# Loading the last batch's q, k and v in three whole transfers, turning one batch on TensorE, and doubling a row buffer in a planned attention-and-mixer kernel

## The chip, the cores and the metric

The kernel runs on one core of a Trainium2 chip. The metric is the device time of one execution in microseconds (us); lower is better. Three runs of the kernel before took 182.30, 182.91 and 182.94 us, median 182.91.

A core has TensorE (PE, matrix products into PSUM, eight banks of 128 x 512 floats), VectorE (DVE), ScalarE (ACT), GpSimd (POOL) and SyncE (SP). Here POOL also issues nearly all loads, since they cast float32 to bf16 on the way, and SP issues the stores, the first loads and all small transfers inside the chip's SBUF memory. Each engine runs its own instructions strictly in order; between engines there are only semaphores.

## What is computed

Four batches of a gated linear attention (8 heads of 48, 768 positions) feed a mixer with a token part and a channel part:

```python
f = sigmoid(f_logit)
for t in range(768):                       # per batch and head
    state = f[t][:, None] * state + outer(k[t], v[t])
    y[t] = q[t] @ state
x = y as (batch, 768, 384)
h = relu(x.T @ w_tok1) @ w_tok2            # over positions
u = x + h.T
out = u + relu(u @ w_ch1) @ w_ch2          # over the 384 channels
```

## The kernel before, in words

**Attention.** A batch is cut into six chunks of 128 positions. `gates` takes `f_logit` through Exp and Ln on ACT and splits the result into two bf16 parts; the subtraction that makes the lower part, `Llo` (L484), runs on DVE for batches 0 and 1, on DVE or POOL for batch 2, on POOL for batch 3. `sums_and_turns` forms running sums over the chunk with a triangular matrix on PE (L553, L554), their exponentials `G` and `Gi` on ACT (L564, L566), scales q and k in one DVE product (L586), and turns the result to `qkT`: on PE with a DVE copy (L603, L616), for batch 3 with a DMA transpose from SP (L593). The last row of the sums is needed down the partitions. ACT writes it to a row of `ends` (L573), and four transfers of SP per chunk (L580) carry it to `glast`, which the state update reads (L649, L652, L654 on DVE). Two copies then put the state into `state_bd` as bf16 (L458 on ACT or L462 on POOL). `attention` handles two chunks at a time: scores (L503), a chunk's own contribution to the state (L519), then per chunk the masking `AmT` (L640) and the output y, from the earlier state (L671) and from within the chunk (L678). It goes to `x_bf` and `x_nat`.

**Mixer.** `mixer` does, per batch: the token part (L708 with `w_tok1`, relu to `h1T` on ACT or DVE; L724 with `w_tok2`), `u` into `x_nat` (L740 on DVE) and as bf16 into `u_bf` (ACT or POOL), the turn of `u` to `uT` in two halves of three tiles, the channel part's first product (L783, 24 groups of three matmuls, relu to `zT` on ACT L467 or DVE L469) and its second (L802, six tiles of twelve matmuls, the last addition on DVE at L808, the store on SP at L812). For a batch listed in `U_TURNED` each half of `uT` is one DMA transpose from SP (L754); otherwise it is nine PE transposes (L765) with three copies out of PSUM (L460).

**Loads.** `load` issues one chunk of one tensor from POOL (L400), 1024 rows of 48 numbers. `load_pair` issues two chunks of f, then k, q, v of each. The buffers of q, k, v are three deep over batches, those of f two, so batch 3 goes into batch 0's q, k, v and batch 1's f. POOL takes its loads in the order in which they are added, and a subtraction or a copy that stands between two loads on POOL holds the later ones.

**The order.** Nothing is issued in source order. Every operation is put into a list (`Plan.add`) with its engines, a rank, what it needs and makes, and an assumed cost; `Plan.order` runs through a model of the engines and hands out operations by earliest start plus lag, then rank, and chooses the engine where an operation may run on several. The table `SHIFTS` overrides rank and lag of several hundred operations by their number in the list. So the position of almost every instruction on every engine follows from the table, and matmuls on a constant tile (L849) fill PE's idle time in the first 25 us.

Below, "batch 2 chunk 5" and the like name these pieces. "Filler" is what PE can do while something else is late, above all the second channel product of the batch before. Line numbers are those of the kernel before; the changed kernel's lines past the table stand six or seven higher.

Of the kernel before, what the change touches and what calls it, by code (L numbers as in the profile page):

```python
# [10 lines left out]
FP32 = mybir.dt.float32  # L11
# [8 lines left out]
U_TURNED = (2,)  # L20
TURNED = 3
SHIFTS = (
# [63 lines left out]
)  # L86
KEPT = 3
SPLIT = 5
# [211 lines left out]
def kernel(  # L300
# [12 lines left out]
    nc = tc.nc  # L313
# [91 lines left out]
    def load_w(name, dst, src, size):  # L405
        add(POOL, 5.0,
            lambda: nc.gpsimd.dma_start(out=dst, in_=src.rearrange("(kt p) n -> p kt n", p=128)),
            make=[name], kind=("load", 900, 1024, size, 8000))
# [424 lines left out]
    for b in range(B):  # L833
# [8 lines left out]
        if b == 1:  # L842
            for c in range(0, NCH, 2):
                load_pair(3, c)
# [38 lines left out]
```

## Time and profile before

| | |
|---|---|
| median of three runs | 182.91 us |
| the profiled execution's own time | 182.56 us |
| its span in the profile | 180.9 us, so 1.66 us lie around it |
| PE busy | 165.9 us (92%) |
| DVE, ACT, POOL busy | 126.3, 122.5, 100.8 us |
| TensorE clock granted | 0.998 |
| POOL's loads by chunk (L400) | 90, about 0.93 us each of POOL's time |
| small transfers to `glast` (L580) | 60, median 4.0 us from issue to landing |
| DMA transposes | 2 of `uT`, 6 of `qkT` |

A busy PE means that at least one matmul is in flight; a matmul of 384 columns is recorded with 0.32 us but the next starts 0.163 us later (28 in 4.71 us). The timeline merges neighbouring instructions of a line. A note in brackets at the end of a line gives the engine's idle time before it and what ended it.

### The profile page before, as it was taken

Reading aid. Unit: us, or ns where it says so; the run is one execution under the profiler, and the core shown is the slowest. Engines: PE = TensorE matmul, PEld = TensorE weight load, DVE = VectorE, ACT = ScalarE, POOL = GpSimd, SP = SyncE. Lnnn points to the kernel's source line nnn. Section 1 sums busy time; section 2 is a strip of 40 time slices with the busy share of each in tenths; the row PEclk is TensorE's granted clock in tenths of the full one; section 3 lists DMA queues with packets and bytes.
Section 4 is the critical chain, followed back from the end, with each engine's and each line's share of the span. In section 5 each row is a group of like instructions: output and inputs, shape, how many; then the busy total and the mean of one; then the engine's idle time right before and its main releaser. Section 6 shows DMA issues by size and latency. Waiting matters only on the chain.

```text
span 180.9 us, 4340 instructions
## 1 busy us (share of the span) xinstructions
PE 165.9 (92%) x1630; PEld 104.3 (58%) x1634; DVE 126.3 (70%) x274; ACT 122.5 (68%) x277; POOL 100.8 (56%) x136
## 2 busy tenths in 40 slices
PE   6978998899989999899999969859999999999992
PEld 2445655566656666566666545536667666656662
DVE  6669995876878998899997978345789455601222
ACT  4578984889869699989989569737827325494100
POOL 7999478795599949879999907420211111000000
PEclk9999999999999999999999999999999999999999
DMA  7999999999999999999999915994395010300132
GB/s 102 137 171 156 147 173 176 202 135 230 131 170 146 210 210 121 153 113 53 159 158 110 182 46 68 106 164 102 64 180 177 4 43 0 124 12 0 43 132 89
DMA packets 106645, 22.15 MB, mean 122 GB/s; under 512 B 99360, under 2 KB 105760, under 8 KB 106624
## 3 DMA queue, kind: packets, MB, share of 16 engines
q0 software_dynamic: 79440, 13.77, 96.7%
q1 hardware_dynamic: 27184, 8.10, 23.0%
q8 instruction: 13, 0.21, 0.5%
q14 instruction: 8, 0.07, 0.1%
HBM read 25.17 MB, written 4.72 MB: 165 GB/s over the span
## 4 chain that ended last, share of the span: by engine, by line
PE 53%; DMA 15%; DVE 11%; ACT 11%; issue 4%; SPq 2%; POOL 1%; ACTq 0%; DVEq 0%; POOLq 0%
PE ps L783 22%; PE ps L802 15%; DMA glast<-ends 8%; DMA uT<-u_bf 4%; DVE AmT L640 3%; PE ps L724 3%; DMA f_sb<-in_f_logit_dram 3%; SPq L580 2%; DVE state L654 2%; ACT state_bd L458 2%; PE ps L708 2%; DVE x_nat L740 2%; PE ps L603 2%; PE ps L765 2%; PE ps L503 2%
## 5 line engine op out<-in xcount | busy, mean ns | idle before, releaser
L783 PE MATMUL ps<-uT,w_ch 128*128 128x384 bf16 x288 | 51.4, 326 | 2.7 <-DMA uT<-u_bf 2.7
L802 PE MATMUL ps<-w_ch,zT 128*128 128x384 bf16 (+2 forms) x300 | 51.8, 320 | 0.0
L467 ACT ACTIVATE zT<-ps 128x384 bf16<-128x384 f32 x72 | 33.9, 491 | 18.4 <-PE ps L783 16.3
L783 PEld LDWEIGHTS <-w_ch 128*128 128x128 bf16 x288 | 27.4, 98 | 20.3 <-issue 2.9
L802 PEld LDWEIGHTS <-zT 128*128 128x128 bf16 x300 | 27.8, 98 | 16.6
L640 DVE TENSOR_TENSOR AmT<-ps,tri_bf 128x512 bf16<-128x512 f32 x46 | 30.2, 684 | 3.8 <-PE ps L503 3.6
L400 POOL DMA_DIRECT2D v_sb<-in_v_dram x24 | 22.2, 927 | 4.5 <-DMA w_ch<-in_moe_w_ch_dram 4.5
L808 DVE TENSOR_TENSOR x_nat<-x_nat,ps 128x384 f32<-128x384 f32 (+2 forms) x25 | 13.3, 535 | 14.3 <-PE ps L802 14.1
L400 POOL DMA_DIRECT2D qk_sb<-in_k_dram x24 | 22.5, 938 | 1.3 <-POOLq L867 0.8
L400 POOL DMA_DIRECT2D qk_sb<-in_q_dram x24 | 22.3, 927 | 0.0
L469 DVE TENSOR_SCALAR zT<-ps 128x384 bf16<-128x384 f32 x24 | 12.9, 554 | 9.8 <-PE ps L783 9.6
L586 DVE TENSOR_TENSOR qk<-qk_sb,GG 128x768 bf16<-128x768 bf16 (+1 forms) x30 | 14.2, 481 | 4.1 <-ACT GG L566 2.2
L400 POOL DMA_DIRECT2D f_sb<-in_f_logit_dram x18 | 16.6, 952 | 0.4 <-DMA f_sb<-in_f_logit_dram 0.2
L478 ACT ACTIVATE f_sb<-f_sb 128x384 f32<-128x384 f32 x24 | 12.5, 520 | 4.6 <-DMA f_sb<-in_f_logit_dram 4.4
L462 POOL CAST state_bd<-state 48x192 bf16<-48x192 f32 x13 | 4.5, 344 | 18.9 <-DVE state L654 9.8
L849 PE MATMUL ps<-steady 128*128 128x512 bf16 x36 | 11.6, 435 | 1.9 <-DVE steady L432 1.5
L458 ACT ACTIVATE state_bd<-state 48x192 bf16<-48x192 f32 x27 | 9.8, 361 | 5.0 <-DVE state L654 4.3
L566 ACT ACTIVATE GG<-ps 128x384 bf16<-128x384 f32 x24 | 11.5, 489 | 1.3 <-PE ps L554 0.9
L564 ACT ACTIVATE GG<-ps 128x384 bf16<-128x384 f32 x24 | 11.6, 487 | 0.9 <-PE ps L554 0.7
L603 PE MATMUL ps<-ident,qk 128*128 128x128 bf16 x144 | 11.7, 220 | 0.6 <-DVE qk L586 0.2
L603 PEld LDWEIGHTS <-qk 128*128 128x128 bf16 x144 | 8.9, 98 | 5.4 <-DVE qk L586 4.0
L740 DVE TENSOR_TENSOR x_nat<-x_nat,ps 128x384 f32<-128x384 f32 x21 | 10.7, 550 | 1.2 <-PE ps L724 1.0
(75 smaller groups left out, 242.9 us busy)
## 6 DMA issues: line engine op xcount, KB each, us to landing
out_dram<-x_nat SPq DMA_DIRECT2D x23, 192.0 KB, 2.0
f_sb<-in_f_logit_dram POOLq DMA_DIRECT2D x18, 192.0 KB, 5.6
qk_sb<-in_k_dram POOLq DMA_DIRECT2D x24, 96.0 KB, 5.2
qk_sb<-in_q_dram POOLq DMA_DIRECT2D x24, 96.0 KB, 5.4
v_sb<-in_v_dram POOLq DMA_DIRECT2D x24, 96.0 KB, 5.5
f_sb<-in_f_logit_dram SPq DMA_DIRECT2D x6, 192.0 KB, 4.7
w_ch<-in_moe_w_ch_dram POOLq DMA_DIRECT2D x2, 576.0 KB, 9.8
w_ch<-in_moe_w_ch_dram POOLq DMA_DIRECT2D x1, 1152.0 KB, 10.2
```

The source lines that it names most:

```text
L400: lambda eng=eng, into=into, of=of: eng.dma_start(out=into, in_=of),
L458: nc.scalar.activation(out_, in_, AF.Copy, bias=0.0, scale=1.0)
L467: nc.scalar.activation(out_, in_, AF.Relu, bias=0.0, scale=1.0)
L469: nc.vector.tensor_scalar(out_, in_, 0.0, None, ALU.max)
L478: add(ACT, r, lambda: nc.scalar.activation(fb, fb, AF.Exp, bias=0.0, scale=-1.0), make=[key], kind=el)
L586: add(DVE, r, lambda n=n: nc.vector.tensor_tensor(qk[i4][:, n, :, 0:D], qk_sb[nb][:, n, :, c, :], GG[i][:, n], ALU.mult), need=[(x, nb, c) ...
L603: nc.tensor.transpose(to[:, o + hp, :], blk(src)[:, hp, :], ident)
L640: add(DVE, r, lambda half=half, made=made: nc.vector.tensor_tensor(half, made(), tb4, ALU.mult), need=["tri_bf"], make=[("AmT", i, p)], ba ...
L740: nc.vector.tensor_tensor(to, un, banks[pm.at][:, 0:DM], ALU.add)
L783: nc.tensor.matmul(banks[pm.at][:, 0:384], lhsT=w[:, kt, c0:c0 + 128], rhs=uT[:, th, :, kt, :], start=(kt == 0), stop=(kt == 2))
L802: nc.tensor.matmul(banks[pm.at][:, 0:n1 - n0], lhsT=zT[:, kt, tt * 128:(tt + 1) * 128], rhs=w_ch2[:, kt, n0:n1], start=(kt == 0), stop=(kt ...
L808: add(DVE, rank("ch2", tt), lambda un=un, pm=pm, n=n1 - n0: nc.vector.tensor_tensor(un, un, banks[pm.at][:, 0:n], ALU.add), make=[("x_nat" ...
```

## The change

Four edits, and a new table:

- `U_TURNED` is empty, so batch 2's `u` is turned by PE.
- Batch 3 is loaded as six chunks of f, then k, q and v whole: three transfers of 6144 rows in place of eighteen of 1024.
- `ends` has four buffers in place of two, so the row of chunk c no longer waits for the transfers of chunk c-2.
- `SHIFTS` is new throughout. (Its numbers also refer to a list that has become three entries shorter.)

```diff
-U_TURNED = (2,)
+U_TURNED = ()
 TURNED = 3
 SHIFTS = (
-    (38,-50,4900), (51,50,3800), (54,300,6100), (87,60,2600), (90,90,400), (91,90,1000), (93,120,800),
...
+    (19,30,1600), (24,60,700), (39,-50,5800), (42,-50,4500), (48,-50,3700), (52,50,4200), (56,300,2900),
...
-    ends = [st([128, H, 64], FP32, f"ends{i}") for i in range(2)]
+    ends = [st([128, H, 64], FP32, f"ends{i}") for i in range(4)]
...
+    def load_whole(b):
+        for n in "kqv":
+            dst, src = names[n]
+            i = b % len(dst)
+            add(POOL, 30.0, lambda into=dst[i], of=src[b].rearrange("h (c t) d -> t h c d", t=C):
+                nc.gpsimd.dma_start(out=into, in_=of), make=[(n, i, c) for c in range(NCH)],
+                kind=("load", 2250, 128 * H * NCH, 4450, 8000))
...
-                ends[i][96:128, :, 0:D], sview()[96:128], AF.Exp, bias=0.0, scale=-1.0),
-                make=[("ends", i)], bank=p_s, kind=el)
+                ends[g4][96:128, :, 0:D], sview()[96:128], AF.Exp, bias=0.0, scale=-1.0),
+                make=[("ends", g4)], bank=p_s, kind=el)
...
-                row = ends[i][127:128].rearrange("o (hp par) d -> o hp (par d)", par=2)
+                row = ends[g4][127:128].rearrange("o (hp par) d -> o hp (par d)", par=2)
...
         if b == 1:
-            for c in range(0, NCH, 2):
-                load_pair(3, c)
+            for c in range(NCH):
+                load("f", 3, c)
+            load_whole(3)
         mixer(b, ranks(b))
```

`g4` is `(b * NCH + c) % 4`, the number that `glast` already uses. In the built programs PE has 18 transposes more and 3 fill matmuls fewer, DVE 8 copies, 7 relus and 2 memsets more and 2 subtractions fewer, ACT 10 instructions fewer, POOL 15 transfers fewer and 2 subtractions and 1 copy more, SP 2 transposes fewer.

More of the change, by code (lines that the diff above doesn't have):

```diff
@@ L439 @@
         once(DVE, lambda i=i: nc.vector.memset(state_bd[i], 0.0), [("sbd", i)], 220)
+    for i in range(4):
         once(DVE, lambda i=i: nc.vector.memset(ends[i][96:128, :, D:64], 1.0), [("ends", i)], 200)
-    for i in range(4):
         for n, tl in (("qh", qh[i]), ("kh", kh[i])):
@@ L573, in sums_and_turns @@
             add(ACT, r, lambda: nc.scalar.activation(
-                ends[i][96:128, :, 0:D], sview()[96:128], AF.Exp, bias=0.0, scale=-1.0),
-                make=[("ends", i)], bank=p_s, kind=el)
+                ends[g4][96:128, :, 0:D], sview()[96:128], AF.Exp, bias=0.0, scale=-1.0),
+                make=[("ends", g4)], bank=p_s, kind=el)
             def across():
-                row = ends[i][127:128].rearrange("o (hp par) d -> o hp (par d)", par=2)
+                row = ends[g4][127:128].rearrange("o (hp par) d -> o hp (par d)", par=2)
                 for hp in range(HP):
                     nc.sync.dma_start(out=glast[g4][:, hp:hp + 1], in_=row[:, hp])
-            add(SP, r, across, need=[("ends", i)], make=[("glast", g4)],
+            add(SP, r, across, need=[("ends", g4)], make=[("glast", g4)],
                 kind=("fix", 1900, (7000, 7000, 4500)[b - 1], 520))
```

122 rows, old and new, of the table SHIFTS are left out of this document.

## The prediction

> **What bounds the kernel.** I read the page's slices first, then PE's timeline for its gaps, the waits, and each gap's cause in the other engines' rows.
>
> ```profile
> PE   6978998899989999899999969859999999999992
> ```
>
> PE is full in nearly every slice of 4.5 us past the start. What stays short is the start (chained through loads, ACT and DVE), slices 23 to 26 (104 to 122 us), and the end. So past 30 us a change pays only by what it takes out of PE's gaps, less what it adds to PE's work. The long gaps in PE's timeline:
>
> ```profile
> 53.32 0.33 PE L671 MATMUL ps<-state_bd,qkT 128*128 128x96 bf16 x4 [0.82 <-ACT state_bd L458]
> 73.92 2.33 PE L724 MATMUL ps<-h1T,w_tok 128*128 128x384 bf16 x12 [0.46 <-ACT h1T L467]
> 105.44 0.33 PE L671 MATMUL ps<-state_bd,qkT 128*128 128x96 bf16 x4 [1.55 <-ACT state_bd L458]
> 112.33 4.71 PE L802 MATMUL ps<-w_ch,zT 128*128 128x384 bf16 x28
> 119.70 4.55 PE L783 MATMUL ps<-uT,w_ch 128*128 128x384 bf16 x27 [2.65 <-DMA uT<-u_bf]
> ```
>
> Others past 30 us are below 0.3 each but one of 0.49; from 119.70 to the last matmul none is listed. The two big ones, 4.20 us together, have their causes here:
>
> ```profile
> 101.01 3.38 POOL L484 TENSOR_TENSOR Llo<-f_sb 128x384 bf16<-128x384 f32 x4
> 102.18 2.44 DVE L654 TENSOR_TENSOR state<-tsum,glast 128x192 f32<-128x192 f32 x1
> 104.65 0.74 ACT L458 ACTIVATE state_bd<-state 48x192 bf16<-48x192 f32 x2 [2.50 <-DVE state L654]
> 112.13 1.90 SPq L754 DMA_TRANSPOSE uT<-u_bf  x1
> ```
>
> A state update that takes 0.36 elsewhere lasts 2.44 while POOL runs four subtractions, so ACT's copies and PE's y of batch 2 chunk 5 are late. Then the DMA transpose, issued at 112.13, lands 7.53 later (the chain has that piece); PE works off 28 matmuls of batch 1 and idles.
>
> **The change, part by part**, against the profiled execution's 182.56. Positions in the changed kernel are from its built order, times by stepping through the pitches of these rows.
>
> *PE turns u of batch 2.* The 2.65 goes: the nine transposes of a half come right after the bf16 copies of u, then 0.35 per copy out of PSUM, and the filler left (12 matmuls before the turns, 8 behind, 20 x 0.163 = 3.3) covers additions, copies and turns. It adds 18 transposes; the chain has nine at batch 3 in 0.50, so +1.0 of PE time, in a stretch that is full. The six DVE copies (six took 1.67 in batch 1) lie beside those 8 and the first L783 groups; uncovered they cost the 1.67. On SP 3.9 of issuing go, for whose followers (transposes of `qkT`) PE does not wait now. Net -1.65; bounds -1.65 and +0.1.
> The Trainium skill ("TensorE: Matmul & The Clock Gate", Part 4: PE-mode transpose) gives about 275 ns for a turn in a kernel; by it 18 would be 4.95 and the sum 185.2. The trace has 0.055 each, pipelined, and decides.
>
> *The late state update.* POOL again has four subtractions of batch 3 in a row (chunks 1, 2, 0, 5), but behind the issue of whole q and, by ACT's order, with gaps; the last state update comes by my steps after them. I take -1.4; bounds -1.55 (gone) and +0.5 (again, and a second run of two in batch 2, whose last subtractions move from DVE to POOL).
>
> *Whole loads: POOL's time.*
>
> ```profile
> 23.16 1.54 POOL L407 DMA_DIRECT2D w_ch<-in_moe_w_ch_dram  x2
> 36.00 1.01 POOL L407 DMA_DIRECT2D w_ch<-in_moe_w_ch_dram  x1
> 84.40 1.80 POOL L400 DMA_DIRECT2D f_sb<-in_f_logit_dram  x2
> ```
>
> The first have 384 rows and take 0.77, a chunk has 1024 and takes 0.90, the last weight 1536 and takes 1.01: 0.208 ns a row. So 6144 rows are an estimated 1.97 (bound from above: six chunks' pitches of 0.87, 5.2). POOL saves 18 x 0.90 - 3 x 1.97 = 10.3, off the path. But half of the state copy for batch 2's last y, on ACT before, is on POOL now, behind the fourth subtraction and whole v: subtraction done at about 103.7, issue 2.0, copy 0.34, y at 106.1, where PE arrives at 105.7. +0.4; bounds 0 and +3.6 (issue 5.2). Behind that copy in POOL's line waits a tile of u_bf, not needed until 112.
>
> *Whole loads: landing.* Before, eight chunk loads start every 6.97 us (84.40, 91.37, 98.35) and land a steady 4.4 after issue, so a chunk drains in 0.87 or less. Two more subtractions and a copy stand in POOL's line ahead of batch 2's last q and v, waiting for ACT's Ln of chunk 5, so f of batch 3 starts near 88.5, not 84.40. Whole q is 18 chunks on: 88.5 + 17 x 0.87 + 4.4 = 107.7. The first product with q (L586) stands on DVE in front of the six additions of u; `G` for it is ready near 108.8. A margin of 1.1. I put +0.3; bounds 0 and +2.5 (at 1.05 a chunk q lands at 110.8, the additions come 2.0 later and PE's filler covers little). v lands by 114, y needs it near 120.
>
> *Four rows of `ends`.*
>
> ```profile
> ACT ends L573 <- DMA glast<-ends: 3.7, 4, 1.2
> ```
>
> ACT's four waits go, but it had no PE gap right behind them: the gap at 53.32 waits for `glast` itself, and the others fall where PE is full. 0; bound -0.5. Two more memsets (0.165 each) stand at 29 us, where DVE waits for PE; 0, or +0.17 if one meets `h1T`.
>
> *The new order.* Three spots. (1) Batch 1's second relu of `h1T` now stands on ACT behind G, Gi and the row of batch 2 chunk 1 (0.37 + 0.53 + 0.50, then 0.45) with 0.94 of PE work beside it: a gap of about 1.2 for 0.46, and two of 0.2 nearby that I no longer find: +0.5, bounds 0 and +0.9. (2) y of batch 1 chunk 1 waits for the same `glast`, but PE arrives with two L783 groups fewer done: +0.3, less 0.2 for a PE turn of batch 0 put off: +0.1, bounds -0.2 and +1.0. (3) The end:
>
> ```profile
> 177.11 0.69 DVE L808 TENSOR_TENSOR x_nat<-x_nat,ps 128x288 f32<-128x288 f32 x2 [0.50 <-PE ps L802]
> ```
>
> Before, the last tile is cut 288 + 96: the final addition takes 0.255, its store of 48 KB 1.6. The changed order does that tile first and ends with a whole one: addition 0.55, store of 192 KB 2.0 at the median. +0.3 + 0.2, hence +0.5, bounds +0.3 and +1.5 (slowest store 2.8). The 3 fill matmuls (0.65) went from PE time that waits anyway.
>
> Sum: -1.65 - 1.4 + 0.4 + 0.3 + 0.5 + 0.1 + 0.5 = -1.25: 181.3. The profiled execution lies 0.35 under the median of its kernel, which the forecast ignores; the comparison is with 182.91.
>
> **Rivals.**
> *A, slower: the whole loads hold up batch 2's u.* If f starts late or the three transfers drain at the 1.0 to 1.3 us a chunk that packet records of batch 3 often show, q lands at 110 to 115, and the DVE products, in order, stand before the six additions, `u_bf`, the turns and every L783 of batch 2. It decides once q lands after about 109.5; from there PE loses one for one. At 1.15 a chunk: 88.5 + 17 x 1.15 + 4.4 = 112.5, 3 later; 181.3 + 3 = 184.3, with POOL's issue at 3 instead of 2 near 185. For it: DMA is the busiest resource there. Against: landings did not lengthen in batch 3, and nothing but stores and small rows competes.
> *B, no change: the order gives it back.* The state updates are held off again and DVE, 13 instructions heavier, opens small PE gaps between 75 and 101, where before has only one of 0.28: 182.56 + 0.1 for the stall kept (-1.25 + 1.4) + 0.3 = 183.0. For it: that stretch has DVE and ACT above 90%, and any misjudged step shows. Against: the same work is only dealt out otherwise.
> The Trainium skill ("SBUF — State Buffer", Who interferes with whom) says that a DVE instruction with two SBUF inputs and a GpSimd one that reads SBUF shut each other out; the 2.44 row agrees, and by it two more subtractions on POOL speak for B.
> *C, more gain:* both gaps go, q is early, and spots (1) and (2) cost nothing: -1.65 - 1.55 + 0.4 + 0.5 = -2.3, and -0.5 for `ends`: 179.8.
> *The edits do not bite* is excluded: the built program has three whole transfers and no DMA transpose of u.
>
> **How the numbers follow.** Forecast 0.42, A 0.25, B 0.22, C 0.11. Predicted: 181.3. For 8 in 10 the range runs from C's far side to A's: 178.9 to 185.2; the forecast's own is 180.3 to 182.4. Of 182.91, 0.5% is 0.9 us, about what a measurement of this kernel can tell from no change: faster means below 182.0, slower above 183.8. Forecast gives 0.38 faster and 0.04 the same; C 0.11 faster; B 0.02, 0.17, 0.03; A slower: faster 0.51, same 0.21, slower 0.28.
>
> **What would show it.** PE's wait for `uT` absent and no idle over 0.5 before batch 2's first L783; whole issues near 2.0 on POOL; q landing before DVE's first batch-3 product (a DVE wait on that DMA means A); no L654 above 0.5 (else B); a wait of L724 on `h1T` near 1.2; PE's last matmul near 175.8 and 3.9 from it to the end of the span. Wrong if PE shows new gaps between 75 and 101 or after 120, where I count none.

## The result: slower, 184.89 us

| kernel | median | kernel before, same chip | ratio to before, 95% interval |
|---|---|---|---|
| changed | 184.89 us (5 runs, 183.81 to 185.98) | 182.55 us (5 runs) | 1.0147 [1.0102, 1.0192] |

The forecast was 181.3, faster. The time lies in its range, the sign is wrong. The ratio leaves disturbed executions out, here and in all that follows, and the medians do not, so the two need not agree to the last tenth.

The changed kernel's profiled execution took 184.89, of which its span is 183.1 (before: 182.56 and 180.9). From its page, the span, the engines' busy time and PE's slices:

```profile
span 183.1 us, 4353 instructions
...
PE 168.0 (92%) x1649; PEld 104.0 (57%) x1649; DVE 130.9 (71%) x289; ACT 117.8 (64%) x267; POOL 93.9 (51%) x124
...
PE   6897996899998999699999889999999999999991
```

PE is busy 2.1 us longer. The hollow at slices 23 to 26 is filled but for two eights, and a new 6 stands at slice 17 (73 to 78 us). PE's timeline in the changed kernel, with the idle time before a row and what ended it in brackets:

```profile
17.33 0.40 PE L609 MATMUL ps<-ident,qk 128*128 128x128 bf16 x4 [1.33 <-DVE qk L592]
...
35.64 4.55 PE L789 MATMUL ps<-uT,w_ch 128*128 128x384 bf16 x27
...
76.13 1.95 PE L730 MATMUL ps<-h1T,w_tok 128*128 128x384 bf16 x11 [1.53 <-ACT h1T L473]
...
100.83 0.33 PE L677 MATMUL ps<-state_bd,qkT 128*128 128x96 bf16 x4 [0.32 <-ACT state_bd L464]
...
102.88 0.62 PE L609 MATMUL ps<-ident,qk 128*128 128x128 bf16 x8 [0.41 <-DVE qk L592]
...
104.94 0.40 PE L509 MATMUL ps<-qkT 48*128 48x128 bf16 x8 [0.30 <-DVE qkT L622]
106.00 0.40 PE L509 MATMUL ps<-qkT 48*128 48x128 bf16 x8 [0.66 <-DVE qkT L622]
...
117.68 1.18 PE L771 MATMUL ps<-ident,u_bf 128*128 128x128 bf16 x18
...
120.00 1.14 PE L789 MATMUL ps<-uT,w_ch 128*128 128x384 bf16 x6
```

The wait of 2.65 for `uT` is gone: 18 transposes in 1.18 and, with filler between, the first hidden-layer product of batch 2 at 120.00 with no idle before it. The other big wait, 1.55 at 105.44, has become four small ones, 1.69 together. New are 1.33 near the start and 1.53 where 0.46 was (batch 1's second token product). What stands behind the four, in the rows of POOL, DVE and ACT:

```profile
90.74 5.31 POOL L398 DMA_DIRECT2D f_sb<-in_f_logit_dram  x6
...
98.20 2.29 POOL L408 DMA_DIRECT2D qk_sb<-in_q_dram  x1
100.43 1.69 POOL L490 TENSOR_TENSOR Llo<-f_sb 128x384 bf16<-128x384 f32 x2
104.87 1.79 POOL L490 TENSOR_TENSOR Llo<-f_sb 128x384 bf16<-128x384 f32 x2 [2.75 <-ACT f_sb L485]
...
98.65 0.90 DVE L660 TENSOR_TENSOR state<-tsum,glast 128x192 f32<-128x192 f32 x1
100.82 1.53 DVE L660 TENSOR_TENSOR state<-tsum,glast 128x192 f32<-128x192 f32 x1 [0.41 <-ACT state_bd L464]
102.28 0.54 DVE L592 TENSOR_TENSOR qk<-qk_sb,GG 128x768 bf16<-128x768 bf16 x1
...
109.77 0.35 DVE L660 TENSOR_TENSOR state<-tsum,glast 128x192 f32<-128x192 f32 x1
...
102.44 0.73 ACT L464 ACTIVATE state_bd<-state 48x192 bf16<-48x192 f32 x2 [1.29 <-DVE state L660]
```

It is the stall of before at another place: POOL starts two subtractions at 100.43, a state update (batch 2 chunk 3) comes at 100.82 and does not end until they have (102.12); all that is behind it on DVE, the q and k product first, is late. The last update of the batch, the one that was held before, comes at 109.77, clear of all four subtractions, and takes 0.35. Behind the 1.53 at 76.13 are these ACT rows, and behind the 1.33 at 17.33 this DVE row:

```profile
74.19 0.49 ACT L570 ACTIVATE GG<-ps 128x384 bf16<-128x384 f32 x1
74.57 0.48 ACT L572 ACTIVATE GG<-ps 128x384 bf16<-128x384 f32 x1
75.08 0.48 ACT L579 ACTIVATE ends<-ps 32x384 f32<-32x384 f32 x1
75.59 0.49 ACT L473 ACTIVATE h1T<-ps 128x384 bf16<-128x384 f32 x1
...
16.91 0.36 DVE L592 TENSOR_TENSOR qk<-qk_sb,GG 128x384 bf16<-128x384 bf16 x1 [1.25 <-DMA qk_sb<-in_k_dram]
```

The relu stands behind G, Gi and the row, as the prediction read from the order. The k product of batch 0's fourth chunk now stands on DVE ahead of work that is ready, and waits for its load.

Where the 2.2 us of the spans come from: 1.04 up to batch 0's first hidden-layer product (34.60, now 35.64); from there PE's listed waits fall from 6.18 to 4.59 (sums of the brackets) while 1.18 of transposes come, -0.4; from the end of the last matmul to the end of the span 3.39 has become 3.81, since a whole tile is stored last, +0.4. The remaining 1.2 or so is not in the listed waits. Between that first product and the last matmul PE is busy 136.41 of 142.91 us before and 138.54 of 143.65 after, so idle time outside the list grew by only 0.2 (0.32 to 0.52). The other 1.0 lies inside PE's busy time, where a late start need not show as idle (a matmul is recorded with 0.32 us, and the next can start after 0.163); no run traces it further.

### The profile page after: what moved, and what is told of

It reads as the page before. It is cut to its first block, busy times and chain, and to the rows that moved or that the text cites. A ratio compares the mean times of both kernels' runs of the same rounds, so it can differ in the third digit from the quotient of the medians.

```text
span 183.1 us, 4353 instructions
## 1 busy us (share of the span) xinstructions
PE 168.0 (92%) x1649; PEld 104.0 (57%) x1649; DVE 130.9 (71%) x289; ACT 117.8 (64%) x267; POOL 93.9 (51%) x124
## 4 chain that ended last, share of the span: by engine, by line
PE 50%; DMA 14%; ACT 8%; POOL 8%; DVE 8%; SPq 5%; issue 4%; DVEq 0%; POOLq 0%; ACTq 0%
PE ps L789 18%; PE ps L808 16%; DMA glast<-ends 9%; SPq L586 5%; POOL qk_sb L398 4%; DMA qk_sb<-in_k_dram 3%; PE ps L714 3%; PE ps L730 2%; ACT state_bd L464 2%; DMA qkT<-qk 2%; PE ps L509 2%; POOL v_sb L398 2%; PE ps L771 2%; DVE state L660 1%; PE ps L609 1%
## 5 line engine op out<-in xcount | busy, mean ns | idle before, releaser
L473 ACT ACTIVATE zT<-ps 128x384 bf16<-128x384 f32 x65 | 31.0, 490 | 17.8 <-PE ps L789 16.2
L475 DVE TENSOR_SCALAR zT<-ps 128x384 bf16<-128x384 f32 x31 | 16.0, 549 | 4.6 <-PE ps L789 4.6
L398 POOL DMA_DIRECT2D v_sb<-in_v_dram x18 | 16.5, 917 | 5.2 <-DMA w_ch<-in_moe_w_ch_dram 5.2
L398 POOL DMA_DIRECT2D qk_sb<-in_k_dram x18 | 16.6, 924 | 1.2 <-POOLq L874 0.8
L398 POOL DMA_DIRECT2D qk_sb<-in_q_dram x18 | 16.6, 921 | 0.0
L468 POOL CAST state_bd<-state 48x192 bf16<-48x192 f32 x15 | 5.1, 341 | 21.1 <-DVE state L660 13.0
L609 PE MATMUL ps<-ident,qk 128*128 128x128 bf16 x144 | 11.1, 220 | 2.6 <-DVE qk L592 2.5
L572 ACT ACTIVATE GG<-ps 128x384 bf16<-128x384 f32 x24 | 11.6, 490 | 1.0 <-PE ps L560 0.7
L464 ACT ACTIVATE state_bd<-state 48x192 bf16<-48x192 f32 x25 | 9.0, 360 | 5.1 <-DVE state L660 3.9
```

Of the source, the lines that this page charges most:

```text
L398: lambda eng=eng, into=into, of=of: eng.dma_start(out=into, in_=of),
L464: nc.scalar.activation(out_, in_, AF.Copy, bias=0.0, scale=1.0)
L473: nc.scalar.activation(out_, in_, AF.Relu, bias=0.0, scale=1.0)
L475: nc.vector.tensor_scalar(out_, in_, 0.0, None, ALU.max)
L609: nc.tensor.transpose(to[:, o + hp, :], blk(src)[:, hp, :], ident)
```

## The experiments

Theory "order": the three structural edits pay, and the new order that the table `SHIFTS` makes costs more than they bring. Rival "edits": the edits cost by themselves. To part them, the experiments have no table: the order of all operations, with engine and PSUM bank, is written out as a list, once as the kernel before has it and once as the changed kernel has it (with either list every engine's instructions and their order are those of the original), and one thing is edited by hand. The source is shorter there, so the lines differ: the state update is L572 to L575, POOL's subtraction L402 to L404, the state copy L376 to L381, the hidden-layer product L702 or L703, the turns of u L685. In the diffs names stand for the operations' numbers: 2.3 is batch 2, chunk 3.

### The old order with the edits put in, together and one by one

```diff
 # e1: all three; e2 the first, e3 the second, e4 the third alone
+DVE  memset ends[2], ends[3]                  behind the first memsets
-SP   DMA transpose uT, tiles 0-2 / tiles 3-5
+PE   9 transposes of u, tiles 0-2             among batch 1's second products (about 112 us)
+PE   9 transposes of u, tiles 3-5             among batch 2's first second products (about 127 us)
+DVE  3 copies to uT behind each nine
-POOL f3.0 f3.1 k q v, k q v, f3.2 f3.3 ...
+POOL f3.0 ... f3.5 at the places of the first six loads, then k3, q3, v3 whole
```

> The kernel before with its order kept instruction by instruction on every engine, and the three edits put into it by hand: batch 2's u turned by TensorE in two groups of nine transposes ahead of the hidden-layer products that read them, f of batch 3 by chunk and then k, q, v whole, four sets of ends rows. Theory 'order' (the loss of the changed kernel comes from the new order that its table of shifts makes, not from the edits): 180.3 to 182.2 us against about 182.5, ratio 0.988 to 0.998; the 2.65 us wait of TensorE for the u transfer is gone and nothing of its size takes its place. Theory 'edits' (the edits cost by themselves, through POOL's issues of 2.3 us, the added transposes and copies, or the two added memsets): 183.0 to 185.0 us, ratio 1.003 to 1.014.

> The order before, with four sets of ends rows and nothing else; two more memsets of about 0.17 us on VectorE, behind the first ones. Theory 'order': no change, ratio 0.998 to 1.002, and the first hidden-layer product of batch 0 starts at 34.6 us as before. Theory 'edits': the two memsets push the start, that product starts at 34.9 us or later, as in the changed kernel (35.6), and the time is 0.3 to 1.0 us longer.

> The order before, with batch 2's u turned by TensorE (18 transposes, six VectorE copies) and nothing else. Theory 'order': 2.65 us of waiting go, 1.2 us of transposes come, 180.8 to 181.8 us, ratio 0.991 to 0.997. Theory 'edits': the copies (six of about 0.35 us) hold up VectorE where it releases batch 3's first chunks, and the gain is given back: 182.2 to 183.5 us.

> The order before, with batch 3's f by chunk first and its k, q, v whole behind, and nothing else; the loads start at the places on POOL where the paired loads started. Theory 'order': between 0.5 us shorter and 0.5 us longer (POOL issues for 6.9 us in place of 16, the first f arrive 2 to 5 us earlier): ratio 0.997 to 1.003. Theory 'edits': the whole k and q arrive after the product that reads their first chunk, or the long issues hold up the state copies behind them: 183.3 to 184.5 us, ratio 1.004 to 1.011.

Measured, on one chip, beside 29 runs of the kernel before with a median of 182.10:

| run | median | ratio to before, 95% interval |
|---|---|---|
| e1, all three | 180.42 us (12 runs) | 0.9906 [0.9849, 0.9962] |
| e2, ends only | 182.77 us (6 runs) | 1.0126 [1.0053, 1.0200] |
| e3, turn only | 181.25 us (12 runs) | 1.0003 [0.9957, 1.0050] |
| e4, whole loads only | 181.11 us (12 runs) | 0.9991 [0.9948, 1.0035] |

The same edits that came with 1.0147 in the new order give 0.9906 in the old one. So the order costs 2.4% against the old one, some 4.4 us (the two intervals together leave an estimated 1.7 to 3.2%), and the edits bring 0.9%: "order" is borne out, "edits" falls. Alone, turn and whole loads are not told from no change by their ratios. For the whole loads that is what "order" expected; for the turn it is a miss, since 0.991 to 0.997 was expected. The four sets alone came out slower by their ratio (by the medians 0.4%), where both theories said nothing or little. Their six times fall into two groups of three, 181.58 to 181.86 and 183.68 to 183.97, and the profile is of one in the lower group, so it cannot show why (span 179.9 against 180.9, batch 0's first hidden-layer product at 33.62; the waits for `uT` are 1.93 and 0.96 where before had one of 2.65). A later pair of runs takes it up.

Why e4 gives little and e1 more can be read in part from the traces; for e3 it stays open. In e3's trace the wait for `uT` is gone and the wait of 1.56 at 105.54 stays; new is one of 1.34 for `state_bd` at 71.30, where before had 0.22. In e1 PE has no wait for `uT`, but the state update is held off again, through all four subtractions. Rows of POOL, DVE and PE in e1, and the POOL and DVE rows of e4 at the same place:

```profile
101.51 3.18 POOL L403 TENSOR_TENSOR Llo<-f_sb 128x384 bf16<-128x384 f32 x4
102.06 2.87 DVE L574 TENSOR_TENSOR state<-tsum,glast 128x192 f32<-128x192 f32 x1
105.74 0.33 PE L591 MATMUL ps<-state_bd,qkT 128*128 128x96 bf16 x4 [1.96 <-ACT state_bd L377]
...
101.19 3.32 POOL L402 TENSOR_TENSOR Llo<-f_sb 128x384 bf16<-128x384 f32 x4
102.26 0.79 DVE L573 TENSOR_TENSOR state<-tsum,glast 128x192 f32<-128x192 f32 x1
```

In e4 `u` still goes by transfer. From the view of the tile `uT` the time from issue to landing of the two transfers, and from PE's timeline the one wait left for them:

```profile
DMA to landing us min/median/max: 2.9/3.1/3.2
...
129.87 2.45 PE L702 MATMUL ps<-uT,w_ch 128*128 128x384 bf16 x14 [1.35 <-DMA uT<-u_bf]
```

Before, the two took 3.5 and 7.5 (the first one had five chunk loads, issued at 110.4 to 113.9, beside it). With whole loads both take about 3, and the wait ahead of batch 2's first product disappears with no turn by PE at all; but PE is then early for the second half and waits 1.35 there. The turn in e1 has neither. In e4's profiled execution the state update took only 0.79, since it got in behind the second of the four subtractions (0.83 each from 101.19; update from 102.26 to 103.05): the same order around it, another outcome, and why is not shown.

### The new order with one thing moved

```diff
 # a1
-ACT  G 2.1, Gi 2.1, ends 2.1, relu h1T 1.1
+ACT  G 2.1, Gi 2.1, ends 2.1
-DVE  relu h1T 1.0
+DVE  relu h1T 1.0, relu h1T 1.1
-PE   transposes 2.0, token product 1.1.5
+PE   token product 1.1.5, transposes 2.0
 # a2
-ACT  state copy 2.3, both halves
+ACT  state copy 2.3, one half
-POOL q3 whole, 4 subtractions of batch 3
+POOL q3 whole, state copy 2.3 (other half), 4 subtractions of batch 3
 # a3
-DVE  k product 0.3, qkT 0.2, tsum 0.1, state 0.1, x_nat 0.1, AmT 0.2, q product 0.3
+DVE  qkT 0.2, tsum 0.1, state 0.1, x_nat 0.1, AmT 0.2, k product 0.3, q product 0.3
```

In a3 the transposes of that k on PE and their copy on ACT go back with it.

> The changed kernel's order, one thing moved: batch 1's second h1T relu goes from ScalarE (behind two gate products and an ends row) to VectorE, right behind the first one, and the last of its six products on TensorE goes ahead of the eight transposes before it. Theory 'order': the wait of 1.53 us ahead of batch 1's second token product is gone or under 0.4 us, that product starts 1.0 to 1.5 us earlier against the first hidden-layer product of batch 0, and the whole is 0.7 to 1.3 us shorter than the changed kernel (183.6 to 184.2 where that takes 184.9). Theory 'edits': no more than 0.3 us of it is left at the end, since another wait behind takes it.

> The changed kernel's order, one thing moved: one half of the state copy behind batch 2's fourth chunk goes from ScalarE to POOL, ahead of the four subtractions of batch 3, so that POOL cannot start them before VectorE's state update is done. Theory 'order' with POOL's subtractions as what holds the update: that update takes 0.35 to 0.45 us in place of 1.53, and TensorE's waits at 100 to 106 us (0.32, 0.41, 0.30, 0.66) fall by 0.8 to 1.4 us together. Rival (the issue of the whole q, not the subtractions, holds the update): it stays above 0.9 us.

> The changed kernel's order, one thing moved: VectorE's k product of batch 0's fourth chunk (which waits 1.25 us for the k load) goes behind the third chunk's scores, with its transposes on TensorE and its copy on ScalarE. Theory 'order': the wait of 1.33 us on TensorE at 17.3 is gone, batch 0's first hidden-layer product starts at 34.4 to 35.0 us in place of 35.64. Rival (the start is set by when the loads land, whatever the order): 35.4 to 35.9 us, the wait goes to another instruction.

One execution each, so the traces count and not the totals (183.44, 182.32 and 184.09 us; the kernel before took 181.27 beside them). a2 first, in the rows of DVE and POOL:

```profile
100.23 0.36 DVE L574 TENSOR_TENSOR state<-tsum,glast 128x192 f32<-128x192 f32 x1 [0.96 <-ACT state_bd L377]
100.75 0.52 POOL L381 CAST state_bd<-state 48x192 bf16<-48x192 f32 x1 [0.84 <-DVE state L574]
101.35 3.18 POOL L403 TENSOR_TENSOR Llo<-f_sb 128x384 bf16<-128x384 f32 x4
```

The copy, which needs the update's result, now stands in POOL's line ahead of the subtractions, so they can no longer meet. The update takes 0.36, and of the four PE waits at 100 to 106 only the 0.32 is left: 1.37 less, as expected. From batch 1's first hidden-layer product to batch 2's the changed kernel needs 39.63, a2 37.95: 1.7 less. The update held for 0.90 took 0.35 here too, at a time when POOL was issuing whole q as before; what had held that one stays open, and the issue alone is not it.

In a1 the wait of 1.53 is gone, but PE's timeline has the next one right behind:

```profile
73.39 2.41 PE L644 MATMUL ps<-h1T,w_tok 128*128 128x384 bf16 x12
...
77.20 0.23 PE L685 MATMUL ps<-ident,u_bf 128*128 128x128 bf16 x1 [0.95 <-ACT u_bf L377]
```

The stage gains 0.4 (from batch 0's first hidden-layer product to batch 1's 44.35 in place of 44.73), not the 1.0 to 1.5 expected: ACT, which was behind all along, is late with the copies of u instead. The reading "1.53 is what the misplaced relu costs" falls.

In a3 the wait of 1.33 is down to 0.20, and its first hidden-layer product starts at 34.70. But a1 and a2, with the front untouched, start at 34.74 and 35.01, because the same k load landed earlier there (DVE waited 0.38 and 0.55 for it, not 1.25). Eight profiled executions with the old front lie at 33.62 to 34.68, three with the new one at 34.74 to 35.64. The old front is better by 0.9 in the mean (34.26 and 35.13), but how much of it the k product's place makes one run does not show.

### All four repairs of the new order, and the best of the old

```diff
 # a4: a1 + a2 + a3, and
-PE/DVE/SP  tile 5 in two pieces, tiles 4, 3, 1, 2, 0
+PE/DVE/SP  tiles 4, 3, 1, 2, 0, tile 5 in two pieces
 # b1: old order, whole loads, four ends, u by transfer, and as in a2 for the last update of batch 2
-ACT  state copy 2.4, both halves
+ACT  state copy 2.4, one half
-POOL 4 subtractions of batch 3
+POOL state copy 2.4 (other half), 4 subtractions of batch 3
 # b2: e1 with b1's edit of the copy; b3: b2 with two sets of ends
```

> The changed kernel's order with four repairs: the three already looked at (second h1T relu of batch 1 on VectorE, one state copy on POOL ahead of batch 3's subtractions, the late k product of batch 0 further back) and the last tile's two pieces stored last again. Theory 'order': from the landmarks of the three looks, 0.4 (front) + 0.4 (h1T, the rest of its 1.5 went to a wait for u_bf) + 1.7 (state update) + 0.4 (tail) = 2.9 us off the changed kernel, so about 182.0 where before takes 182.5, ratio 0.994 to 1.002. Theory 'edits': the order is not what costs, the ratio stays above 1.008.

> The order before with four ends rows and the whole loads, batch 2's u still by the transfer, and one half of the state copy behind batch 2's fifth chunk on POOL ahead of batch 3's subtractions. Theory 'the whole loads already free the u transfer' (it lands in about 3 us once no small loads run beside it): no wait of TensorE for the u transfer, no state wait near 105 us, 177.5 to 179.5 us where before takes 182, ratio 0.973 to 0.986, faster than with the turn by TensorE. Rival (the turn is needed): a wait of 1 us or more ahead of batch 2's first hidden-layer product, ratio above 0.990.

> The order before with all three edits (as in the first of these runs), and one half of the state copy behind batch 2's fifth chunk on POOL ahead of batch 3's subtractions. Theory 'POOL's subtractions hold the state update, and the two u transfers' waits are removed together only by the turn': no wait on TensorE for the u transfers (the version without the turn still waited 1.35 to 2.19 us for the second one), the wait of 1.96 us at 105.7 gone, 178.0 to 179.5 us where before takes 182.3, ratio 0.975 to 0.985, the fastest of all. Rival (the held copies only move the wait to the sums that read the subtractions): a new TensorE wait of 1 us or more between 105 and 112, ratio 0.988 to 0.994 as without it.

> The fastest version so far (old order, turn by TensorE, whole loads, POOL's subtractions held) with two sets of ends rows in place of four; two memsets fewer, nothing else. It tells what the four sets are worth, which alone came out 1.3% slower without a trace of it in the profile. Theory 'the four sets are worth nothing': ScalarE waits again 2.8 to 3.7 us for the small transfers, TensorE does not, ratio 0.979 to 0.988 as with four (0.983). Theory 'the four sets cost' (their transfers land late and scattered, as VectorE's waits of 2.2 and 0.9 us for glast in the version with four suggest): ratio 0.970 to 0.978, and those waits fall below 0.6 us. Theory 'they gain': ratio 0.990 or more.

| run | median | before, same chip | ratio to before, 95% interval |
|---|---|---|---|
| a4, new order mended | 183.04 us (12 runs) | 183.35 us | 1.0028 [0.9986, 1.0070] |
| b1, old order, no turn, held | 182.29 us (12 runs) | 183.35 us | 1.0003 [0.9959, 1.0048] |
| b2, old order, all three, held | 179.23 us (6 runs) | 182.50 us | 0.9832 [0.9766, 0.9897] |
| b3, as b2 with two ends | 179.99 us (6 runs) | 182.40 us | 0.9879 [0.9821, 0.9937] |

a4: the repairs take the ratio from 1.0147 to 1.0028, 1.2% or 2.2 us; expected were 2.9. In its profiled execution the state update takes 0.36 again (103.26). That execution, at 186.77 the longest of the twelve, has batch 0's first hidden-layer product at 37.72, so it shows nothing of the repair of the front. Against e1, half of what the new order costs is found, and 1.2% stays open. The fairer mark is b2, where the subtractions are held too: from it to a4 it is 2.0%, all of it open.

b1: in its profiled execution the state wait is gone and the span is 178.0, but PE waits 2.19 for the second transfer of `u`, and the ratio is no better than before: the theory that the whole loads make the turn needless fell, and its rival held, though the wait came ahead of the second half and not ahead of the first product.

b2 beats both kernels, 1.7% under the kernel before. Rows of DVE, POOL and PE in its profiled execution:

```profile
104.41 0.36 DVE L574 TENSOR_TENSOR state<-tsum,glast 128x192 f32<-128x192 f32 x1 [0.90 <-DMA glast<-ends]
105.33 3.19 POOL L403 TENSOR_TENSOR Llo<-f_sb 128x384 bf16<-128x384 f32 x4
108.57 0.32 PE L474 MATMUL ps<-Llo,tri_bf 128*128 128x384 bf16 x1 [0.28 <-POOL Llo L403]
...
54.72 0.33 PE L591 MATMUL ps<-state_bd,qkT 128*128 128x96 bf16 x4 [2.37 <-ACT state_bd L377]
```

The update takes 0.36, and the subtractions, 4 us later than in e1, cost PE 0.28 where their result is read. What is left is at 54.72: batch 1's first update waited 2.18 for a small transfer to `glast`. That is not the four sets' doing, since in b3, with two, DVE waits 2.05 at the same update; and e1, with the order of b2 up to there, has 0.67 in place of the 2.37, so the landing differs from execution to execution. b2 and b3 are not told apart (their intervals overlap), so four sets are worth nothing that shows, and e2's 1.3% is not seen again in this pair.

## Why the prediction was wrong

*Turn by PE: right in the trace.* -1.65 was counted; the wait of 2.65 went and 18 transposes took 1.18, so -1.47. By the Trainium skill's price ("TensorE: Matmul & The Clock Gate", Part 4: PE-mode transpose), about 275 ns each in a kernel, an estimate for them is 4.95; the 0.066 each of this trace is far below it, as the prediction chose. What was not seen is that the whole loads end the first of the two waits by themselves. As time, the turn shows only in company: alone it gave 1.0003 (e3), with whole loads and held subtractions it takes 1.0003 (b1) to 0.9832 (b2).

*The late state update: the step that failed.* -1.4 was taken because "the last state update comes by my steps after them". That sentence came true (109.77, 0.35 long), but the step asked only about the last update and left out the one before it. Its times were early, too: f of batch 3 started at 90.74, not 88.5, and an issue of 6144 rows took 2.25 to 2.29, not 1.97. By the steps POOL would have been free for the first two subtractions at about 97.7 (an estimate: 88.5 + 6 x 0.87 + 2 x 1.97); they began at 100.43. There they met that earlier update, which took 1.53, and PE's waits there are 1.69 for 1.55: +0.1 in place of -1.4. Whether an earlier f alone would have kept them apart no run shows, since ACT had the input of the second one ready only at 100.53. a2 shows the cause: with the two kept apart by POOL's own line the update takes 0.36 and the stage is 1.7 shorter. The meeting of two engines was worked out from times that were off by 2.7 here, 2.2 of it in the start of f, at a point where 0.4 us of order decided. The bound of +0.5 was the end to stay near.

*The new order: mis-sized.* Of +1.1 for three spots, the end came out right (+0.5 counted, 0.42 in the trace). The relu's gap grew by 1.07 for 0.5 counted, though a1 says that its place alone is worth 0.4. The front, where I took 0.2 off for a PE turn put off, is later by 1.04 in this execution and 0.9 in the mean: the k product in front of ready work on DVE was not looked for. The +0.3 of spot (2) was not paid: the wait of 0.82 went, and 0.28 and 0.53 came (53.01 and 56.82). And beyond the spots the order costs about 1 us that no listed wait shows: e1 against the changed kernel is 2.4% for the same edits, a4's four repairs bring back half. Counting large gaps one by one missed the rest.

*Whole loads.* POOL's issues were 0.3 longer each than estimated. The copy for batch 2's last y was released on POOL at 110.25 by DVE's update (L660), not by POOL's line, so the +0.4 was not paid where it was put. Whole q did land late, 12.0 after issue at 110.20, where 107.7 was counted and rival A's mark was 109.5. But DVE took its first product with it only at 113.72, behind a wait of 0.65 for `GG` and not for q, so +0.3 was not paid either, and rival A, a late q that holds up u, is out.

*Ends.* 0 was counted; b2 against b3 agrees, while e2's 1.3% stays unexplained.

*Rival B* had the mechanism, the state updates held off again, and too small a price: 183.0, where the front, the relu's gap and what no listed wait shows made it 184.89. The Trainium skill's rule beside it ("SBUF — State Buffer", Who interferes with whom), that a VectorE instruction with two SBUF inputs and a GpSimd instruction that reads SBUF shut each other out, agrees with 1.53, 2.44 and 2.87 against 0.36 in a2.

## What to carry to other kernels

When a change brings a new order with it, put the edits into the old order by hand before judging them: here the edits were worth 0.9% and the order cost 2.4%. Where two engines must not run at the same time, do not leave it to durations: put an instruction that needs the one engine's result into the other's line, ahead of what must wait (one moved copy did it here: the update fell from 2.87 to 0.36, and the ratio from 0.991 to 0.983, though those two intervals overlap). A wait that goes is worth what the next wait in that stage lets through: the relu's 1.53 was worth 0.4, the first `uT` wait nothing in b1, where the second took its place.

## What the runs showed of the hardware that was not expected

- A state update that meets POOL's subtractions waits through what is left of the run, back to back: 1.53 for two, 2.44 when it met the second of four (before), 2.87 when it met the first (e1), 0.36 without. Once, in e4, it met the second and got in ahead of the third (0.79).
- A DMA transpose of half of `u` landed 7.5 us (before) and 6.8 us (e2) after issue with five loads by chunk beside it, and 2.9 to 4.7 us without (before, e2, e4, b1).
- POOL's issue of 6144 rows took 2.21 to 2.29 us where 1024 rows take about 0.9.
- The start varies by about a microsecond between executions with the old front (33.62 to 34.68). In the changed kernel's front it went with the landing of one k load (34.74, 35.01 and 35.64 for DVE waits of 0.38, 0.55 and 1.25). So a single profile cannot price an edit there.
